# q and k in tiles of 256, 256 and three times 512 tokens in a fused attention and gMLP kernel, with E's zeros partly on ScalarE and a new order

## The chip, the cores and the metric

The kernel runs on one core of a Trainium2 chip. Its engines are TensorE (PE; its weight loads PEld), VectorE (DVE), ScalarE (ACT), GpSimd (POOL) and SyncE (SP), which issues all of this kernel's DMAs; each takes its instructions in the order in which they were written, and they wait for each other by semaphores. The metric is the device time of one execution in microseconds (us), as a median of several runs.

## The reference

One sequence of 2048 tokens with 448 channels goes through two blocks with residuals. The first is attention of 16 heads of 28 channels, where each token looks at 8 positions: itself and those 2, 4, ... 14 back. The second is a gMLP: a GELU layer of 2 x 896 channels, whose second half is normalised and mixed over all tokens by a 2048 x 2048 matrix. All data is bf16.

```python
qkv = layernorm(x) @ wqkv                   # 448 -> 3*448
idx = pos[:, None] - 2 * arange(8)          # masked where negative
attn = softmax(q . k[idx] * 28 ** -0.5)
h = x + (attn . v[idx]) @ wo
z = gelu(layernorm(h) @ w_in)               # 448 -> 1792
z1, z2 = z[:, :896], layernorm(z[:, 896:])
out = h + (z1 * (w_sp @ z2 + b_sp)) @ w_out
```

## The kernel before

The tokens lie in 16 blocks of 128 (`x_tm`). Each block is normalised on VectorE (statistics L634 and L636, GpSimd's rstd L628 and L629, `xn` L645) and transposed into `xhT`: the first four blocks (`xT0` to `xT3`) by TensorE (L674) with an eviction (`xe`), the others by a transposing DMA.

q and k come from `product` (L502), in 5 tiles of tokens (`QT`) times 4 groups of heads (`make_qk`, job `qk<tile>_<group>`). A product has 14 matmuls on half the rows of the array, in two jobs A (8) and B (6) with another job between them, and takes two of the 8 PSUM banks: k in one, q in the other. `qe` copies k to `kT` (L512), `qf` copies q to `qd` twice, each time with other rows masked by `qm` (ScalarE, L723), or in one instruction on VectorE (L726). Weights come packed: `wraw` is loaded in two halves, and ten copies `wp` bring it into `wqk` (L512), where GpSimd has zeroed the gaps (`wpad`, L695). `kT` and `qd` are a ring of 1592 tokens; tile 4 is written over the first tokens' places once blocks 0 to 4 have been used, and blocks 14 to 17 of the attention read it there.

The attention has 18 blocks of 112 to 128 queries. For each: logits `lg` (L814, 16 matmuls), exponentials `ex` into one of four slots of `E` (ScalarE, L824 and L825), a mask product `mk` (VectorE, L832), the product with the values `o` (L845, two jobs of 16), reciprocal and scaling (`rc`, `om`, L862 and L865) into `otm`, a small copy `od`, and a transposing DMA into `OT`. Values are products too (`v`, 14 matmuls of 448 columns, for two blocks), evicted by `ve`. E's unused halves must be zero: `pads0` to `pads3` (L598 and L599) write them once. Blocks 11 to 17 need one more copy `oc` behind their DMA.

Then `y` (with wo), the residual `h` (L775), the second normalisation, z1 and z2 (L502 again, 512 and 448 columns; GELU at L946, L902 and L905; `z2c` evicts z2 where its GELU comes later), the token mixing `g` (L974, 448 matmuls of 512 columns from `wsp_la`, `wsp_lb`, `wsp_hi`, which transposing DMAs bring), bias and product with z1 (L983, L986), the output product `wo` (L998), the last residual (L1005) and 16 stores.

No scheduler runs when the kernel is built: every job has a number, `ORDER` lists all numbers in the order in which they are given out (926 is a filler matmul, L1013, that keeps TensorE busy), `BANK` the PSUM banks, and `ON` the engine of the jobs that have a choice. `Sched.issue` derives the waits from what each instruction reads and writes.

Of the kernel before, what the change touches and what calls it, by code (L numbers as in the profile page):

```python
# [1073 lines left out]
```

## Time and profile before

| what | us |
|---|---|
| median of 3 runs | 241.84 (241.83 to 242.95) |
| the profiled execution: its time | 242.61 |
| its span | 240.9 |
| TensorE busy | 230.7 |
| VectorE, ScalarE, GpSimd busy | 147.3, 92.5, 32.4 |

The granted TensorE clock is 1.00 throughout. A line of the profile names a source line, an engine and an operation with its result and operands; a matmul's busy time reaches to its modelled end, so that neighbours overlap. Timeline lines begin with start and length; a bracket at the end gives the idle time before the line and what ended it.

### The profile page before, as it was taken

What the parts mean: (1) busy time and instruction counts of PE and PEld (TensorE: products, weight loads), DVE (VectorE), ACT (ScalarE), POOL (GpSimd) and SP (SyncE); (2) the same over time, 40 slices, a digit from 0 to 9 for tenths busy, and PEclk for the clock granted to TensorE, in tenths of its full rate; (3) what the DMA queues carried; (4) which work ended last, traced back from release to release, by engine and by line L of the source; (5) the groups of instructions that cost most, each with busy time, mean ns of one, the idle gap of its engine ahead of it and who ended that gap; (6) DMA issues with size and microseconds to landing.
All of it is one profiled execution on the core that took longest, in us unless ns stands there. A gap on an engine that the chain in (4) does not pass through costs nothing.

```text
span 240.9 us, 5622 instructions
## 1 busy us (share of the span) xinstructions
PE 230.7 (96%) x2394; PEld 115.7 (48%) x2406; DVE 147.3 (61%) x335; ACT 92.5 (38%) x132; POOL 32.4 (13%) x80
## 2 busy tenths in 40 slices
PE   7769899999999999999999999999999999999995
PEld 2536555555565554444444444444444434444443
DVE  6997787889997969677794044620311741052844
ACT  2588958868789474989800000000000000000000
POOL 5553210111132030303333000000000000000000
...
GB/s 181 373 80 103 90 112 71 135 197 118 114 110 132 114 135 182 95 180 171 180 191 198 189 105 3 0 0 0 3 1 0 0 38 3 0 19 19 38 79 114
DMA packets 66313, 23.31 MB, mean 97 GB/s; under 512 B 58608, under 2 KB 66160, under 8 KB 66288
## 3 DMA queue, kind: packets, MB, share of 16 engines
...
q8 instruction: 19, 0.31, 0.6%
...
## 4 chain that ended last, share of the span: by engine, by line
PE 87%; DVE 6%; ACT 5%; issue 1%; POOL 0%; POOLq 0%
PE psum L974 37%; PE psum L502 35%; PE psum L998 9%; PE psum L845 3%; ACT qd L723 2%; PE psum L814 2%; DVE ub L983 2%; DVE z1p L986 1%; ACT kT L512 1%; PE psum L1013 1%; DVE E L598 1%; DVE st L634 1%; ACT E L824 1%; DVE x_tm L775 0%; ACT xhT L512 0%
## 5 line engine op out<-in xcount | busy, mean ns | idle before, releaser
L983 DVE TENSOR_TENSOR ub<-psum,bb 128x512 bf16<-128x512 f32 x28 | 19.3, 690 | 56.1 <-PE psum L974 55.8
L974 PE MATMUL psum<-wsp_hi,z2p 128*128 128x512 bf16 x217 | 50.1, 379 | 0.7 <-DVE srg L1005 0.4
L974 PEld LDWEIGHTS psum<-wsp_hi,z2p 128*128 128x128 bf16 x224 | 21.8, 98 | 26.9 <-DVE srg L1005 0.6
L502 PE MATMUL psum<-xhT,wqk 64*128 64x512 bf16 (+3 forms) x280 | 27.4, 335 | 0.0
L974 PE MATMUL psum<-wsp_la,z2p 128*128 128x512 bf16 x110 | 26.4, 379 | 0.3 <-issue 0.2
L974 PE MATMUL psum<-wsp_lb,z2p 128*128 128x512 bf16 x110 | 26.2, 379 | 0.1
L502 PE MATMUL psum<-w_in,hnT 64*128 64x448 bf16 x224 | 24.1, 349 | 0.0
L502 PE MATMUL psum<-hnT,w_in 64*128 64x512 bf16 x196 | 24.0, 376 | 0.0
L998 PE MATMUL psum<-w_out,z1p 128*128 128x448 bf16 (+1 forms) x119 | 22.8, 342 | 0.1
L909 DVE BATCH_NORM_STATS2 st<-z2p 128x6 f32<-128x448 bf16 x32 | 18.5, 612 | 1.6 <-ACT z2p L905 1.4
L723 ACT ACTIVATE qd<-psum,qm 128x512 bf16<-128x512 f32 (+3 forms) x34 | 18.1, 615 | 3.5 <-PE psum L502 3.4
L634 DVE BATCH_NORM_STATS2 st<-x_tm 128x6 f32<-128x448 bf16 x32 | 19.0, 611 | 0.1
L825 ACT ACTIVATE E<-psum 128x1024 bf16<-128x1024 f32 x17 | 17.0, 1031 | 1.3 <-PE psum L814 0.7
L974 PEld LDWEIGHTS psum<-wsp_lb,z2p 128*128 128x128 bf16 x112 | 10.9, 98 | 13.2
L974 PEld LDWEIGHTS psum<-wsp_la,z2p 128*128 128x128 bf16 x112 | 10.9, 98 | 13.3 <-DVE mv L912 0.4
L629 POOL TENSOR_TENSOR rs<-rs,negh 128x2 f32<-128x2 f32 (+2 forms) x22 | 16.9, 767 | 1.8
L502 PE MATMUL psum<-wv,xhT 64*128 64x448 bf16 x126 | 15.0, 351 | 1.9 <-ACT kT L512 1.9
L998 PEld LDWEIGHTS psum<-w_out,z1p 128*128 128x128 bf16 x119 | 11.5, 98 | 10.4 <-DVE z1p L986 0.4
L1005 DVE TENSOR_TENSOR srg<-psum,x_tm 128x448 bf16<-128x448 f32 (+1 forms) x17 | 9.7, 593 | 10.9 <-PE psum L998 9.3
L502 PEld LDWEIGHTS psum<-xhT,wqk 64*128 64x128 bf16 x280 | 12.3, 94 | 8.3 <-DVE wqk L512 0.4
L502 PEld LDWEIGHTS psum<-w_in,hnT 64*128 64x128 bf16 x224 | 10.7, 94 | 10.5 <-ACT z1p L946 0.2
L645 DVE TENSOR_SCALAR xn<-x_tm,mv,rs 128x512 bf16<-128x512 bf16 x32 | 12.5, 416 | 4.6 <-POOL rs L629 3.9
(65 smaller groups left out, 238.3 us busy)
## 6 DMA issues: line engine op xcount, KB each, us to landing
...
out_dram<-srg SPq DMA_DIRECT2D x16, 112.0 KB, 1.7
...
```

The source lines that it names most:

```text
L502: ins = e.matmul(out(k), w(k, p0, c), x(k, p0, c), start=(k, p0, c) in first, stop=(k, p0, c) in last, tile_position=(p0, 0))
L629: (lambda e: e.tensor_tensor(R, A, negh[:, 0:1].to_broadcast([128, n]), ALU.pow), [rr, r_negh], r_rs[k][m:m + n])],
L634: [(lambda e: e.bn_stats(st[:, m, :], src), [rsrc], [r_st[k][m]])], dve_t(D))
L645: [(lambda e: e.tensor_scalar(xn[:, s, :].rearrange("p (a b) -> p a b", a=2), bass.AP(x_tm[:].tensor, m * D, [[NB * D, 128], [192, 2], [1, ...
L723: return e.activation(qd[:, g, i, a:a + n], psv(tk, 0, n), AF.Copy, scale=qm[:, i:i + 1])
L825: return e.activation(o[:, :, :, 0:64], psum[:, tk.b * 512:tk.b * 512 + 1024].rearrange("p (i h q) -> p i h q", i=2, q=64), AF.Exp, scale= ...
L845: ins = e.matmul(psum[:, c:c + DH + 1], E[64 * r:64 * r + 64, slot, a:a + 128], V1[64 * r:64 * r + 64, vs, 4 * (2 * k + gg) + hh, 0:DH + 1 ...
L909: [(lambda e, m=m, k=k: e.bn_stats(st3[:, m, k, :], z2p[:, m, D * k:D * (k + 1)]), [r_z2[m]], [r_st[2][m]])], dve_t(D))
L974: ins = e.matmul(psv(tk), z2p[:, s, 128 * fc:128 * fc + 128], w[:, 512 * (tc % 2):512 * (tc % 2) + 512], start=(s == 0), stop=(s == NB - 1))
L983: [(lambda e, tc=tc, s=s, tk=tk: e.tensor_tensor(ub[:, s, :], psv(tk), bb[:, 512 * tc:512 * tc + 512], ALU.add), [r_bb], [r_ub[s]])], dve_ ...
L998: ins = e.matmul(psv(tk, 0, c1 - c0), z1p[:, fc, 128 * m:128 * m + 128], w_out[:, fc, c0:c1], start=(fc == 0), stop=(fc == FC7 - 1))
L1005: [(lambda e, m=m, s=s, tk=tk, c0=c0, c1=c1: e.tensor_tensor(srg[:, s, c0:c1], psv(tk, 0, c1 - c0), x_tm[:, m, c0:c1], ALU.add), [r_x[m]], ...
```

## The change

- The tiles of q and k are tokens 0, 256, 512, 1024 and 1536 onwards, 256, 256, 512, 512 and 512 wide. Before, they began at 0, 256, 568, 1080 and 1578, and were 256, 312, 512, 512 and 470 wide. Tile 1 now needs token blocks 2 and 3 alone, where it needed block 4 too.
- Tile 4 now begins inside the part of the ring that isn't reused: its first 56 tokens go to their own places, 1536 to 1591, for block 13 of the attention, and its tokens from 1578 on go to the ring's start. So each of its evictions is two instructions, of 470 and of 56 columns, and 14 of its columns are written twice.
- E's zeros may be written by ScalarE, as an activation with scale 0 of `warm`: `pads0` and `pads1` are now there, `pads2` on GpSimd, `pads3` on VectorE. Before, three were on VectorE and `pads1` on GpSimd.
- `ORDER`, `BANK` and `ON` are new tables. By `ON`, VectorE now has q of tile 0, group 3, k of tile 1, group 0 and q of tile 1, group 1, five evictions of z2 (`z2c`) where it had one, one eviction of the values (`ve12`), and `od0` to `od4`, `od7`, `od12`, `od14`, `od16` and `od17`.

There are now 16 fillers where there were 21. SyncE's first 13 loads stand as before.

TensorE from its first instruction. `warm` is the filler's operand, `ident` and `xn` those of a transpose, `xhT` and `wqk` those of q and k, `wv` of the values, `qd` and `kT` of the logits. Before:

```order
1 L1013 MATMUL psum<-warm 128x512 x12
2 L674 MATMUL psum<-ident,xn 128x128 x8
3 L1013 MATMUL psum<-warm 128x512 x7
4 L502 MATMUL psum<-xhT,wqk 128x256 x56
5 L1013 MATMUL psum<-warm 128x512
6 L502 MATMUL psum<-wv,xhT 128x448 x8
7 L674 MATMUL psum<-ident,xn 128x128 x8
8 L502 MATMUL psum<-wv,xhT 128x448 x6
9 L1013 MATMUL psum<-warm 128x512
10 L502 MATMUL psum<-wv,xhT 128x448 x8
11 L814 MATMUL psum<-qd,kT 64x2x78 x8
```

The same place now:

```order
1 L1036 MATMUL psum<-warm 128x512 x8
2 L682 MATMUL psum<-ident,xn 128x128 x4
3 L1036 MATMUL psum<-warm 128x512
4 L682 MATMUL psum<-ident,xn 128x128 x4
5 L1036 MATMUL psum<-warm 128x512 x7
6 L502 MATMUL psum<-xhT,wqk 128x256 x56
7 L682 MATMUL psum<-ident,xn 128x128 x8
8 L502 MATMUL psum<-wv,xhT 128x448 x8
9 L502 MATMUL psum<-xhT,wqk 128x256 x30
10 L502 MATMUL psum<-wv,xhT 128x448 x6
11 L502 MATMUL psum<-xhT,wqk 128x256 x26
12 L502 MATMUL psum<-wv,xhT 128x448 x8
```

The second pair of transposes (rows 7) moved ahead of all value products, and the whole second tile of q and k stands among them, without fillers.

VectorE from its first instruction. `st_62` and `mv_63` are the statistics of the first normalisation, `rs_68` its rstd. Before:

```order
1 L588 MEMSET warm 128x512
2 L603 MEMSET otm 128x512
3 L598 MEMSET E 128x16x32
4 L599 MEMSET E 128x32
5 L598 MEMSET E 128x16x32
6 L599 MEMSET E 128x32
7 L601 MEMSET qm 128x2
8 L602 MEMSET qm 32x1 x4
9 L634 BN_STATS st_62<-x_tm 128x6
10 L636 BN_AGGR mv_63<-st_62 128x2
11 L634 BN_STATS st_62<-x_tm 128x6
12 L636 BN_AGGR mv_63<-st_62 128x2
```

The same place now:

```order
1 L588 MEMSET warm 128x512
2 L642 BN_STATS st_62<-x_tm 128x6
3 L644 BN_AGGR mv_63<-st_62 128x2
4 L642 BN_STATS st_62<-x_tm 128x6
5 L644 BN_AGGR mv_63<-st_62 128x2
6 L653 TENSOR_SCALAR xn<-x_tm,mv_63,rs_68 128x512 x2
7 L603 MEMSET E 128x16x32
8 L603 MEMSET E 128x32
9 L512 COPY wqk<-wraw 128x2x8x28 x2
10 L611 MEMSET otm 128x512
11 L512 COPY wqk<-wraw 128x2x4x28 x3
12 L609 MEMSET qm 128x2
```

The statistics of blocks 0 and 1 moved to the head; one slot of E, otm and qm are cleared behind them, among the copies of the weights. Behind this come the statistics of blocks 3, 2, 7 and 5, the normalisation of blocks 2 and 3, statistics of 4 and 6, and then q of tile 0, group 3.

ScalarE at the evictions of tile 4, with the exponentials (`E`) of blocks 8 and 12 at its two ends. Before, its four groups stood apart:

```order
35 L723 ACTIVATE qd<-psum,qm 128x470 x2
36 L512 ACTIVATE kT<-psum 128x470
37 L825 ACTIVATE E<-psum 128x16x64
38 L512 ACTIVATE V_81<-psum 128x32x28
39 L825 ACTIVATE E<-psum 128x16x64 x3
40 L512 ACTIVATE V_81<-psum 128x32x28
41 L825 ACTIVATE E<-psum 128x16x64
42 L512 ACTIVATE V_81<-psum 128x32x28
43 L512 ACTIVATE kT<-psum 128x470
44 L723 ACTIVATE qd<-psum,qm 128x470 x4
45 L512 ACTIVATE kT<-psum 128x470
46 L825 ACTIVATE E<-psum 128x16x64
```

Now:

```order
43 L848 ACTIVATE E<-psum 128x16x64 x3
44 L731 ACTIVATE kT<-psum 128x470
45 L731 ACTIVATE kT<-psum 128x56
46 L737 ACTIVATE qd<-psum,qm 128x470 x2
47 L737 ACTIVATE qd<-psum,qm 128x56 x2
48 L731 ACTIVATE kT<-psum 128x470
49 L731 ACTIVATE kT<-psum 128x56
50 L737 ACTIVATE qd<-psum,qm 128x470 x2
51 L737 ACTIVATE qd<-psum,qm 128x56 x2
52 L731 ACTIVATE kT<-psum 128x470
53 L731 ACTIVATE kT<-psum 128x56
54 L848 ACTIVATE E<-psum 128x16x64
```

Two groups and the k of a third now come in a row between exponentials, each with its pieces of 56 columns; that group's q and the fourth group follow the last row shown.

The diff, cut to its core:

```diff
-ORDER = [21, 45, 22, 28, 23, 25, 30, 0, 31, 32, 27, 46, 33, 121, 47, 1, 53, 54, 44, 48, 34, 49, 2, 26, 124, 55, 56, 926, 926,
+ORDER = [21, 45, 30, 0, 44, 46, 24, 47, 22, 31, 32, 33, 1, 53, 54, 48, 23, 55, 2, 121, 123, 49, 56, 26, 122, 124, 926, 926,
...
-QT = [(0, 256), (256, 568), (568, 1080), (1080, 1592), (1578, 2048)]
+QT = [(0, 256), (256, 512), (512, 1024), (1024, 1536), (1536, 2048)]
...
-        r_qk = [[spot("qk%d_%d" % (t, g), o_qk, 12 * SL * 2) for g in range(12)] for t in range(len(QT))]
+        r_qk = [[spot("qk%d_%d" % (t, g), o_qk, 12 * SL * 2) for g in range(24 if t == 4 else 12)] for t in range(len(QT))]
...
-            move_z("pads%d" % i, [(lambda e, i=i: e.memset(ez(i), 0.0), [], [r_Ez[i]]),
+            def zero(e, o, act):
+                if act:
+                    x = warm[:, 0:64]
+                    return e.activation(o, x if len(o.shape) == 2 else x.unsqueeze(1).to_broadcast([128, NHEAD, 64]), AF.Copy, scale=0.0)
+                return e.memset(o, 0.0)
+            za = ON.get("pads%d" % i) == "act"
...
-                move("qe%d_%d" % (t, g), "act", ekey, lambda n=n, a=a, g=g: kT[:, g, a:a + n], lambda n=n, tk=tk: psv(tk, 1, n),
...
+                parts = [(0, lo, n)] if t < 4 else [(1578 - lo, 0, hi - 1578), (0, lo, SL - lo)]
+
+                def ke(e, part, eng, g=g, tk=tk):
+                    c, a, w = part
+                    o, x = kT[:, g, a:a + w], psv(tk, 1, 512)[:, c:c + w]
+                    return e.activation(o, x, AF.Copy) if eng == "act" else e.tensor_copy(o, x)
+
+                def qe(e, part, i, eng, g=g, tk=tk):
+                    c, a, w = part
+                    x = psv(tk, 0, 512)[:, c:c + w]
+                    if eng == "act":
+                        return e.activation(qd[:, g, i, a:a + w], x, AF.Copy, scale=qm[:, i:i + 1])
+                    return e.tensor_tensor(qd[:, g, :, a:a + w], x.unsqueeze(1).to_broadcast([128, 2, w]),
+                                           qm[:].unsqueeze(2).to_broadcast([128, 2, w]), ALU.mult)
...
-                if (t == 4 if b >= 14 else t < 4 and lo < t0 + nq and hi > t0 - pad):
+                if (t == 4 if b >= 14 else lo < t0 + nq and hi > t0 - pad):
```

More of the change, by code (lines that the diff above doesn't have):

```diff
@@ L25 @@
 LOOK = {'pe': 0.009410205530073946, 'act': 1e-09, 'dve': 0.19498114580727732, 'pool': 1e-09, 'sp': 0.13408016923274957}
-ORDER = [21, 45, 22, 28, 23, 25, 30, 0, 31, 32, 27, 46, 33, 121, 47, 1, 53, 54, 44, 48, 34, 49, 2, 26, 124, 55, 56, 926, 926,
[40 rows of a table removed]
-BANK = [2, 0, 4, 5, 4, 6, 2, 0, 2, 6, 0, 4, 6, 2, 0, 6, 4, 0, 4, 0, 0, 0, 4, 0, 6, 4, 2, 6, 4, 0, 2, 2, 0, 6, 6, 0, 2, 4, 4,
[3 rows of a table removed]
+ORDER = [21, 45, 30, 0, 44, 46, 24, 47, 22, 31, 32, 33, 1, 53, 54, 48, 23, 55, 2, 121, 123, 49, 56, 26, 122, 124, 926, 926,
[40 rows of a table added]
+BANK = [0, 2, 0, 1, 2, 0, 4, 6, 6, 0, 0, 2, 2, 4, 6, 6, 0, 2, 2, 6, 4, 6, 0, 0, 2, 4, 4, 0, 4, 0, 0, 4, 2, 6, 0, 6, 2, 4, 0,
[3 rows of a table added]
     7]
@@ new lines @@
+ON = {'pads0': 'act', 'pads1': 'act', 'pads2': 'pool', 'pads3': 'dve', 'xe0_0': 'act', 'xe0_1': 'act', 'xe1_0': 'act',
+    'xe2_0': 'act', 'xe3_0': 'act', 'wp0_0_0': 'dve', 'wp0_1_0': 'act', 'wp0_0_2': 'dve', 'wp0_1_2': 'act', 'wp1_0_0':
+    'dve', 'wp1_1_0': 'dve', 'wp1_0_1': 'dve', 'wp1_1_1': 'act', 'wp1_0_2': 'act', 'wp1_1_2': 'act', 'qe0_0': 'act',
[4 rows of a table added]
+    'qf3_2': 'dve', 'qe3_3': 'act', 'qf3_3': 'act', 've0': 'act', 'padsx': 'dve', 'od0': 'dve', 'od1': 'dve', 've2':
+    'act', 'od2': 'dve', 'od3': 'dve', 've4': 'act', 'od4': 'dve', 'od5': 'pool', 've6': 'act', 'qe4_0': 'act',
+    'qf4_0': 'act', 'qe4_1': 'act', 'qf4_1': 'act', 'qe4_2': 'act', 'qf4_2': 'act', 'qe4_3': 'act', 'qf4_3': 'act',
+    'od6': 'pool', 'od7': 'dve', 've8': 'act', 'od8': 'pool', 'od9': 'pool', 've10': 'act', 'od10': 'pool', 'od11':
+    'pool', 'oc11': 'dve', 've12': 'dve', 'od12': 'dve', 'oc12': 'dve', 'od13': 'pool', 'oc13': 'dve', 've14': 'act',
+    'od14': 'dve', 'oc14': 'act', 'od15': 'pool', 'oc15': 'act', 've16': 'act', 'od16': 'dve', 'oc16': 'act', 'od17':
+    'dve', 'oc17': 'dve', 'z2c1': 'dve', 'z2c2': 'dve', 'z2c3': 'act', 'z2c4': 'dve', 'z2c5': 'act', 'z2c6': 'act',
+    'z2c7': 'dve', 'z2c8': 'act', 'z2c9': 'dve', 'z2c10': 'act', 'z2c13': 'act'}
@@ L597, in bass_sequential_preLN__sliding_local_dilated__mixer_gmlp__prompt_kernel @@
         for i in range(NE):
-            move_z("pads%d" % i, [(lambda e, i=i: e.memset(ez(i), 0.0), [], [r_Ez[i]]),
-                                  (lambda e, i=i: e.memset(E[:, i, NHEAD * 128:NHEAD * 128 + 64], 0.0), [], [r_Ez[i]])], {"dve": 0.65, "pool": 1.3})
+            def zero(e, o, act):
[4 more added lines that the diff above has]
+            za = ON.get("pads%d" % i) == "act"
+            move_z("pads%d" % i, [(lambda e, i=i, za=za, zero=zero: zero(e, ez(i), za), [r_warm], [r_Ez[i]]),
+                                  (lambda e, i=i, za=za, zero=zero: zero(e, E[:, i, NHEAD * 128:NHEAD * 128 + 64], za), [r_warm], [r_Ez[i]])],
+                   {"dve": 0.6, "pool": 1.1, "act": 1.05})
         r_qm = Res("qm")
@@ L705, in make_qk @@
             lo, hi = QT[t]
-            n, a = hi - lo, lo if t < 4 else 0
+            n = hi - lo
             for g in range(4):
@@ L716, in make_qk @@
                 ekey = lo / 112.0 + KEY["qe"] + KEY["qkg"] * g
-                move("qe%d_%d" % (t, g), "act", ekey, lambda n=n, a=a, g=g: kT[:, g, a:a + n], lambda n=n, tk=tk: psv(tk, 1, n),
-                     [], [r_qk[t][3 * g]] + [r_qk[o][3 * g] for o in also], evac_t(n), [tk], (tk, 1, 1))
-                name = "qf%d_%d" % (t, g)
-                eng = ON.get(name, "act")
-                def fa(e, i, n=n, a=a, g=g, tk=tk):
-                    return e.activation(qd[:, g, i, a:a + n], psv(tk, 0, n), AF.Copy, scale=qm[:, i:i + 1])
@@ L725, in fv @@
-                def fv(e, n=n, a=a, g=g, tk=tk):
-                    return e.tensor_tensor(qd[:, g, :, a:a + n], psv(tk, 0, n).unsqueeze(1).to_broadcast([128, 2, n]),
-                                           qm[:].unsqueeze(2).to_broadcast([128, 2, n]), ALU.mult)
-                wr = [[r_qk[o][3 * g + 1 + i] for o in (t,) + tuple(also)] for i in range(2)]
-                ops = [(lambda e, i=i, fa=fa: fa(e, i), [r_qm], wr[i]) for i in range(2)] if eng == "act" else [(fv, [r_qm], wr[0] + wr[1])]
@@ new lines, in qe @@
+                def qe(e, part, i, eng, g=g, tk=tk):
[5 more added lines that the diff above has]
+                                           qm[:].unsqueeze(2).to_broadcast([128, 2, w]), ALU.mult)
+                for name, bank in (("qe", 1), ("qf", 0)):
+                    name = "%s%d_%d" % (name, t, g)
+                    eng = ON.get(name, "act")
+                    ops, durs = [], {"act": 0.0, "dve": 0.0}
+                    for ip, part in enumerate(parts):
+                        w = part[2]
+                        wr = [[r_qk[t][12 * ip + 3 * g + i]] + [r_qk[o][3 * g + i] for o in also if ip == 0] for i in range(3)]
+                        if bank:
+                            ops.append((lambda e, part=part, eng=eng, ke=ke: ke(e, part, eng), [], wr[0]))
+                            durs = {"act": durs["act"] + act_t(w), "dve": durs["dve"] + dve_t(w)}
+                        else:
+                            ops += [(lambda e, part=part, i=i, eng=eng, qe=qe: qe(e, part, i, eng), [r_qm], wr[1 + i] if eng == "act" else wr[1] + wr[2])
+                                    for i in (range(2) if eng == "act" else [0])]
+                            durs = {"act": durs["act"] + 2 * act_t(w) + 0.187, "dve": durs["dve"] + dve_t(2 * w)}
+                    j = pl.job(name, eng, ekey, ops, durs[eng], use=[tk], rel=(tk, bank, 1))
+                    j.alts = durs
```

14 lines of the change are left out of this document (removed), and 94 rows, old and new, of tables (BANK, ON, ORDER).

## The prediction

> **What bounds the kernel now.** I read the page first, then busy time by stretch, then the timeline of the first 30 us and the groups of instructions.
>
> ```profile
> span 240.9 us, 5622 instructions
> PE 230.7 (96%) x2394; PEld 115.7 (48%) x2406; DVE 147.3 (61%) x335; ACT 92.5 (38%) x132; POOL 32.4 (13%) x80
> PE   7769899999999999999999999999999999999995
> ```
>
> TensorE is busy nearly throughout; what is missing stands in the first five slices of 6 us. The next view gives stretches: start and end, length, then busy us of PE, PEld, DVE, ACT and POOL.
>
> ```profile
> 9.78:30.00 20.22, 17.04 (x318) 10.76 (x320) 16.29 (x46) 17.62 (x37) 7.21 (x17) 1.00 0.48 123
> 30.00:119.70 89.70, 89.21 (x1498) 47.27 (x1496) 74.46 (x170) 70.33 (x88) 14.97 (x34) 1.00 0.81 137
> 119.70:238.40 118.70, 117.58 (x556) 54.99 (x565) 48.69 (x97) 1.24 (x2) 4.15 (x8) 1.00 0.24 49
> 48.00:72.00 24.00, 23.60 (x558) 13.68 (x554) 22.32 (x53) 18.38 (x25) 4.04 (x10) 1.00 0.71 134
> ```
>
> From 30 us to the last matmul, 208.4 us, TensorE idles 1.6 us. So a new order can gain there next to nothing; it can gain only ahead of 30 us, and it can lose anywhere. The front, engine by engine (start, length, engine, line, what; in brackets what the engine waited for):
>
> ```profile
> 1.51 4.78 PE L1013 MATMUL psum<-warm 128*128 128x512 bf16 x12 [1.51 <-DVE warm L588]
> 7.72 0.62 PE L674 MATMUL psum<-ident,xn 128*128 128x128 bf16 x8 [1.42 <-DVE xn L645]
> 8.18 1.67 PE L1013 MATMUL psum<-warm 128*128 128x512 bf16 x7
> 9.78 3.23 PE L502 MATMUL psum<-xhT,wqk 64*128 64x256 bf16 x56
> 14.41 0.93 PE L502 MATMUL psum<-wv,xhT 64*128 64x448 bf16 x8 [1.39 <-ACT kT L512]
> 17.57 0.39 PE L1013 MATMUL psum<-warm 128*128 128x512 bf16 x1 [1.01 <-ACT qd L723]
> 19.95 3.87 PE L502 MATMUL psum<-xhT,wqk 64*128 64x312 bf16 x56
> ```
>
> Real work starts with the first q/k tile at 9.78. Up to 30 us the idle time is 20.22 - 17.04 = 3.2 us, and the filler at 17.57 hides another 0.3: 3.5 us of holes. The two large ones come after the first q/k tile: all eight banks hold its products, and TensorE waits until ScalarE has emptied them (kT, qd); the second q/k tile, which could fill the time, needs token block 4, which comes late through a transposing DMA.
>
> **The change, part by part.** The sum is made against the profiled execution's 242.61 us (span 240.9, 1.7 around it); the median of the runs is 241.84, 0.77 lower, and I take the same difference off both.
>
> *When real work starts.* The rows on which this rests:
>
> ```profile
> 0.79 0.87 SPq L527 DMA_DIRECT2D x_tm<-in_A_x_dram  x2
> DMA to landing us min/median/max: 2.1/5.7/6.9
> 3.91 0.63 DVE L634 BATCH_NORM_STATS2 st<-x_tm 128x6 f32<-128x448 bf16 x1
> 5.77 0.41 DVE L645 TENSOR_SCALAR xn<-x_tm,mv,rs 128x512 bf16<-128x512 bf16 x1 [0.29 <-POOL rs L629]
> 6.88 0.64 POOL L605 MEMSET V<- 128x96 bf16 x1
> 6.98 0.68 DVE L645 TENSOR_SCALAR xn<-x_tm,mv,rs 128x512 bf16<-128x512 bf16 x1
> 7.76 0.95 POOL L598 MEMSET E<- 128x1024 bf16 x1
> L512 DVE COPY wqk<-wraw x5: 242/264/957, 6.8 to 9.4; 128x448 bf16<-128x448 bf16 x4, 128x224 bf16<-128x224 bf16 x1
> L598 DVE MEMSET E<- 128x512 uint32 x3 | 1.5, 485 | 0.2
> 7.94 0.86 ACT L512 ACTIVATE wqk<-wraw 128x224 bf16<-128x224 bf16 x2 [5.66 <-DMA wraw<-in_A_wqkv_dram]
> L825 ACT ACTIVATE E<-psum 128x1024 bf16<-128x1024 f32 x17 | 17.0, 1031 | 1.3 <-PE psum L814 0.7 <-PE psum L845 0.5
> ```
>
> Before, VectorE clears otm, two slots of E and qm ahead of the first statistics, which start at 3.91. Now they start when x lands, 0.8 + 2.1 = 2.9, and the first xn, which ends 2.3 us after that start (5.77 + 0.41 - 3.91), ends at 5.2; the second one GpSimd round later, at about 6.3 (5.77 to 6.98 is such a round). Then VectorE clears one slot of E (0.5 and a small memset: to 6.9) and packs wqk. In that time GpSimd, whose rstd ends near 5.7, has the memset of wqk's gaps, a mask step and the clearing of slot 2 (0.95) in its queue, so that this last one runs from about 6.7 to 7.7. In the rows an xn of 0.41 takes 0.68 under one GpSimd memset and a copy of 0.26 takes 0.96 under the other: I take the first copy as held until 7.8. The second ends at 8.1, otm's memset at 8.6, and the three small copies (0.24 each; the second half of wraw has landed at 7.9) at 9.35. The first product needs two of them: 9.2. Without the hold it would be 8.6, the other bound; the third bound is no gain, 9.8. I take 9.2, the row that shows a copy under this very memset: **-0.6** (-1.2 to 0). ScalarE's two clearings (1.03 each by the E row of the same 1024 columns, and small ones) run from 2.3 (7.94 - 5.66) to about 4.8, inside its 5.66 of waiting; uncovered they would cost 2.5.
>
> *The fillers.* The same filler takes 4.78/12 = 0.40 at first and 1.67/7 = 0.24 later, with a granted clock of 1.00 in both, so the column doesn't show this. Now 8 run ahead of the first transposes, ending near 4.9, with short waits of 0.3 behind; I count that as warm enough (0). The Trainium skill, "TensorE: Matmul & The Clock Gate", Part 1, says the array runs at half rate until a free-running window of about 3.4 us was busy, and that the moment differs between runs. By that rule 8 fillers might not be enough; that is a rival below.
>
> *The holes behind the first tile.* The rows:
>
> ```profile
> 9.58 0.61 DVE L634 BATCH_NORM_STATS2 st<-x_tm 128x6 f32<-128x448 bf16 x1
> 11.54 0.72 POOL L629 TENSOR_TENSOR rs<-rs,negh 128x2 f32<-128x2 f32 x1
> 11.64 1.57 ACT L723 ACTIVATE qd<-psum,qm 128x256 bf16<-128x256 f32 x4 [1.06 <-PE psum L502]
> 13.08 1.23 ACT L512 ACTIVATE kT<-psum 128x256 bf16<-128x256 f32 x4
> 15.70 1.08 ACT L512 ACTIVATE xhT<-psum 128x512 bf16<-128x512 f32 x2 [0.67 <-PE psum L674]
> L983 DVE TENSOR_TENSOR ub<-psum,bb 128x512 bf16<-128x512 f32 x28 | 19.3, 690 | 56.1 <-PE psum L974 55.8
> ```
>
> The second tile is now tokens 256 to 511, which TensorE itself transposes, so its 56 matmuls (3.2) stand where the holes were. First hole: the first tile ends at 9.2 + 3.2 = 12.4. VectorE sets qm (0.5 after 9.35) and starts the statistics of blocks 2 and 3 at 9.9; from that start to their rstd it is 11.54 + 0.72 - 9.58 = 2.7, so 12.6; their xn may again meet a GpSimd memset (V's ones are next there): 13.3. Hole 0.9, at best 0.3. The transposes, their eviction (two in 1.08) and the first value product last to 14.8; a q/k product to 15.3. Second hole: the next one's banks hold the first tile's group 3, whose q now leaves by VectorE, behind two normalisations, two statistics of 0.6 and four aggregations: from 15.2 to 15.9 (0.69 by the row of the like read of PSUM). Hole 0.65. Behind that ScalarE's queue (0.39 for a qd, 0.31 for a kT by the two rows above) is one step ahead of or behind TensorE; I count 0.65 of small waits at the first logits and the third value product. In all 2.2 for 3.5: **-1.3**; bounds -2.3 (0.3, 0.6 and small ones of 0.3) and 0 (as many holes as before).
>
> *Columns.* Three widths of 56 matmuls are in rows:
>
> ```profile
> 113.40 6.21 PE L502 MATMUL psum<-hnT,w_in 64*128 64x512 bf16 x56
> ```
>
> 3.23, 3.87 and 6.21 for 256, 312 and 512 are 12.1 to 12.6 ns a column, so 14 columns fewer are **-0.2**. Two more separate groups of logits (14 for 12) put back **+0.1**, by the 0.42 below against their 0.29 in pairs; both within ±0.3.
>
> *Tile 4.* Its eviction writes 470 columns and then 56 again: 12 more instructions on ScalarE. And its four groups now stand close together. From the logits of block 8 on, ScalarE has three exponentials and all four groups before the logits of block 13 can run; value and output products wait behind those on TensorE.
>
> ```profile
> L512 ACT ACTIVATE kT<-psum 128x470 bf16<-128x470 f32 x4 | 2.2, 562 | 0.4 <-PE psum L502 0.4
> L723 ACT ACTIVATE qd<-psum,qm 128x470 bf16<-128x470 f32 x8 | 4.8, 650 | 1.7 <-PE psum L502 1.7
> L512 ACT ACTIVATE wqk<-wraw 128x224 bf16<-128x224 bf16 x3 | 1.2, 388 | 5.7 <-DMA wraw<-in_A_wqkv_dram 5.7
> 27.07 1.96 ACT L825 ACTIVATE E<-psum 128x1024 bf16<-128x1024 f32 x2
> 53.41 1.49 PE L502 MATMUL psum<-wv,xhT 64*128 64x448 bf16 x14
> 52.85 0.42 PE L814 MATMUL psum<-qd,kT 64*64 64x128 bf16 x16
> 66.72 0.99 PE L845 MATMUL psum<-V,E 64*128 64x29 bf16 x64
> ```
>
> TensorE meanwhile has 3.4 q/k groups (6.21/4 each: 5.3), three products of 1.45, one logits (0.4) and four blocks of 32 E matmuls (0.5 each by 0.99 for 64): about 12. ScalarE: 3 x 1.03 + 4 x 0.56 + 8 x 0.65 = 10.5, less 0.1 an instruction where they follow each other (two exponentials of 1.03 take 1.96), plus 12 small ones. No row has 56 columns. A kT takes in sequence 0.46 for 470 columns (0.56 less 0.1) and 0.31 for 256 (1.23/4), 0.7 ns a column, which leaves 0.17 for 56; the upper bound is the 0.39 of 224 columns. So 10.5 - 1.5 + 2.0 = 11 against 12: covered, **0**; upper bound 10.5 + 4.7 = 15.2, a wait of 3.2.
>
> *Everything else* moves banks, engines and queue places at stretches where TensorE idles 1.6 in 208: one value eviction, four evictions of z2 and two small copies more go to VectorE, which idles 89.70 - 74.46 = 15.2 there, while SyncE's queue keeps its first 13 loads. **0**, from -0.4 (half of today's late holes gone) to +1.4.
>
> Sum: -0.6 - 1.3 - 0.2 + 0.1 = **-2.0**: 242.61 becomes 240.6, and the median 241.84 becomes **239.8**.
>
> **The rivals.**
>
> *Better.* The copies aren't held and the holes shrink to their lower bounds: -1.2 - 2.3 - 0.1 = -3.6, 238.2; more likely half-way, 238.7. Chance 0.10.
>
> *Cold array.* If the wait ahead of the transposes keeps the array slow for one more window, the 7 later fillers take 2.8 instead of 1.7 from 6.6 on and end at 9.4, and part of the first tile runs at 0.40/0.24 of its time: 0.3 to 1.4, say 0.8. Result 240.6. For it: the ratio in the rows. Against: 8 fillers are 3.2 us, nearly the whole of the 4 or so that 12 needed. Chance 0.08.
>
> *VectorE takes the lead back.* Between 48 and 72 us it is busy 22.32 of 24. An added eviction of 896 columns there costs 1.06:
>
> ```profile
> L512 DVE CAST z2p<-psum 128x896 bf16<-128x896 f32 x1 | 1.1, 1057 | 0.0
> ```
>
> If the whole of it and two small copies (0.15 each) reach TensorE, 1.4 of 2.0 is lost: 241.2, no change. Against: by the sums above VectorE has done by 30 us what it does today by then, and four evictions of q and k more (0.4 to 1.2 each), so it has a lead of its own. Chance 0.14.
>
> *ScalarE is late with tile 4* (slower). Where a small piece costs its full 0.39 and nothing overlaps, block 13's logits wait 3.2; where ScalarE enters that place with 1 us of arrears, 4.2, and the result is 239.8 + 3.2 to 4.2, 243.0 to 244.0, say 243.5. It decides from about 0.35 a piece on; below 0.2 it costs nothing. For it: ScalarE has little slack there, 18.4 busy of 24, and gets 2 to 4.7 us more. Chance 0.10.
>
> **How the numbers follow.** The forecast, with its own range of 239.0 to 240.6, has 0.58. A measurement of this kernel tells 0.5%, 1.2 us, from no change: faster than 240.63 are the forecast and the better case, 0.68; within, the cold array and VectorE, 0.22; slower, ScalarE, 0.10. The range of 8 in 10 leaves out the far side of the better case and the slower one: 238.3 to 242.0.
>
> **What would show it.** Right: the first q/k product starts between 8.6 and 9.4; TensorE has 1.5 to 2.5 us of holes from there to 30 us, the first before the transposes of blocks 2 and 3, the second before a q/k product that waits for VectorE's qd; a piece of 56 columns shows under 0.3; from 30 us on TensorE idles under 2. Wrong: fillers at 0.40 behind 6 us; matmuls of L837 or of values waiting for ScalarE's kT or qd of 56 columns; waits for VectorE at E's products above 1 us; or a first tile that starts no earlier than 9.8.

## The result and the profile after

The changed kernel takes 241.35 us (median of 13 runs, 239.48 to 243.81) beside 242.33 us (13 runs, 241.83 to 242.95) for the kernel before on the same chip: ratio 0.9937, 95% interval 0.9915 to 0.9960, 1.5 us less. (Four of its runs, at 243.4 to 243.8 with a mean granted clock of 0.993, are left out of the ratio; with them, the medians stand at 0.9960, 1.0 us less.) Run again later on another chip it had 0.9953 (0.9927 to 0.9979). The prediction was 239.8 us, a gain of 2.0, in a range of 238.3 to 242.0. The profiled execution took 241.03 us, 1.58 less than before. Its page:

```profile
span 239.3 us, 5622 instructions
PE 230.0 (96%) x2401; PEld 115.9 (48%) x2401; DVE 151.7 (63%) x339; ACT 91.7 (38%) x141; POOL 30.8 (13%) x77
```

The stretches, as before (start and end, length, busy us of PE, PEld, DVE, ACT and POOL, granted clock):

```profile
8.41:30.00 21.59, 19.09 (x336) 11.60 (x338) 19.15 (x55) 17.38 (x36) 6.49 (x17) 1.00 0.55 142
30.00:119.70 89.70, 88.19 (x1484) 47.41 (x1479) 80.36 (x181) 66.45 (x93) 16.11 (x35) 1.00 0.79 137
119.70:236.70 117.00, 116.99 (x563) 54.71 (x561) 46.78 (x90) 1.69 (x2) 2.81 (x6) 1.00 0.23 48
```

Up to 30 us TensorE idles 21.59 - 19.09 = 2.5 us, where it had 3.5 us of holes. But in the middle stretch it now idles 1.5 us, where it had 0.5. The timeline of TensorE says where (in brackets the idle time ahead of a row and what ended it):

```profile
6.52 1.67 PE L1036 MATMUL psum<-warm 128*128 128x512 bf16 x7
8.41 3.23 PE L502 MATMUL psum<-xhT,wqk 64*128 64x256 bf16 x56 [0.22 <-DVE wqk L512]
12.46 0.83 PE L682 MATMUL psum<-ident,xn 128*128 128x128 bf16 x8 [0.82 <-DVE xn L653]
15.08 1.37 PE L502 MATMUL psum<-xhT,wqk 64*128 64x256 bf16 x22 [0.44 <-DVE qd L738]
20.96 0.93 PE L502 MATMUL psum<-wv,xhT 64*128 64x448 bf16 x8 [0.29 <-ACT E L848]
23.82 1.04 PE L502 MATMUL psum<-xhT,wqk 64*128 64x512 bf16 x8 [0.91 <-ACT E L848]
49.60 1.04 PE L502 MATMUL psum<-xhT,wqk 64*128 64x512 bf16 x8 [1.10 <-DMA xhT<-xn]
```

The first q/k product starts at 8.41 instead of 9.78. Four holes follow. And at 49.60 stands a wait that the kernel before doesn't have: tile 4's first product waits 1.10 us for a transposing DMA. SyncE's queue shows the reason (start, time that the queue was taken):

```profile
40.64 3.59 SPq L526 DMA_TRANSPOSE OT<-otm  x2
44.28 2.58 SPq L526 DMA_TRANSPOSE xhT<-xn  x2
```

The transposes of blocks 15 and 14 (`xhT<-xn`) stand behind those of outputs 3 and 4 (`OT<-otm`), which VectorE has to write first. In the kernel before, blocks 12 to 15 stood ahead of output 2, and the last three of them went out here:

```profile
35.46 5.33 SPq L526 DMA_TRANSPOSE xhT<-xn  x3
```

Next, VectorE at the head of the changed kernel, and ScalarE's groups of the small pieces:

```profile
2.90 0.63 DVE L642 BATCH_NORM_STATS2 st<-x_tm 128x6 f32<-128x448 bf16 x1 [1.45 <-DMA x_tm<-in_A_x_dram]
6.89 0.73 DVE L512 COPY wqk<-wraw 128x448 bf16<-128x448 bf16 x2
9.00 0.63 DVE L642 BATCH_NORM_STATS2 st<-x_tm 128x6 f32<-128x448 bf16 x1
```

```profile
L737 ACT ACTIVATE qd<-psum,qm 128x56 bf16<-128x56 f32 x8 | 2.2, 365 | 0.0
L731 ACT ACTIVATE kT<-psum 128x56 bf16<-128x56 f32 x4 | 1.0, 258 | 0.0
```

The statistics of block 0 start when x lands, and those of blocks 2 and 3 at 9.00 instead of 9.58. Two milestones split the time: the first product with the spatial weights (118.54; before 119.77) and the end of the last matmul. Here are the rows of after, then of before:

```profile
118.54 1.69 PE L997 MATMUL psum<-wsp_la,z2p 128*128 128x512 bf16 x7
228.48 8.21 PE L1021 MATMUL psum<-w_out,z1p 128*128 128x448 bf16 x49
```

```profile
119.77 1.46 PE L974 MATMUL psum<-wsp_la,z2p 128*128 128x512 bf16 x6 [0.16 <-issue]
230.07 8.22 PE L998 MATMUL psum<-w_out,z1p 128*128 128x448 bf16 x49
```

From the first q/k product to the first milestone it is 109.99 before and 110.13 after: what the smaller holes bring, the new wait takes. From there to the end of the last matmul it is 118.52 and 118.15. So the 1.6 us are 1.37 at the start and 0.4 late, less 0.1 between.

### The profile page after: what moved, and what is told of

It is laid out like the page before. It is cut to its first block, busy times and chain, and to the rows that moved or that the text cites. A ratio compares the mean times of both kernels' runs of the same rounds, so it can differ in the third digit from the quotient of the medians.

```text
span 239.3 us, 5622 instructions
## 1 busy us (share of the span) xinstructions
PE 230.0 (96%) x2401; PEld 115.9 (48%) x2401; DVE 151.7 (63%) x339; ACT 91.7 (38%) x141; POOL 30.8 (13%) x77
## 3 DMA queue, kind: packets, MB, share of 16 engines
HBM read 6.83 MB, written 1.84 MB: 36 GB/s over the span
## 4 chain that ended last, share of the span: by engine, by line
PE 77%; DVE 11%; ACT 5%; DMA 2%; POOL 2%; issue 1%; SPq 1%; POOLq 0%; DVEq 0%
PE psum L997 40%; PE psum L502 24%; PE psum L1021 9%; DVE st L642 3%; PE psum L868 2%; PE psum L837 2%; DMA xhT<-xn 2%; POOL rs L637 2%; DVE xn L653 1%; DVE x_tm L798 1%; ACT z1p L969 1%; DVE otm L888 1%; DMA x_tm<-in_A_x_dram 1%; DVE z2p L512 1%; ACT qd L737 1%
## 5 line engine op out<-in xcount | busy, mean ns | idle before, releaser
L997 PE MATMUL psum<-wsp_hi,z2p 128*128 128x512 bf16 x224 | 51.8, 379 | 0.0
L502 PE MATMUL psum<-xhT,wqk 64*128 64x512 bf16 (+1 forms) x280 | 28.0, 334 | 2.7 <-DMA xhT<-xn 1.1
L997 PE MATMUL psum<-wsp_la,z2p 128*128 128x512 bf16 x112 | 25.7, 379 | 0.0
L737 ACT ACTIVATE qd<-psum,qm 128x256 bf16<-128x256 f32 (+3 forms) x38 | 17.8, 555 | 2.3 <-PE psum L502 2.1
L969 ACT ACTIVATE z1p<-psum 128x1024 bf16<-128x1024 f32 x14 | 13.9, 1023 | 12.1 <-PE psum L502 12.1
L868 PEld LDWEIGHTS psum<-V,E 64*128 64x128 bf16 x576 | 12.2, 93 | 6.9 <-DVE otm L888 0.4
```

The costliest lines, as they stand in the source:

```text
L502: ins = e.matmul(out(k), w(k, p0, c), x(k, p0, c), start=(k, p0, c) in first, stop=(k, p0, c) in last, tile_position=(p0, 0))
L737: return e.activation(qd[:, g, i, a:a + w], x, AF.Copy, scale=qm[:, i:i + 1])
L868: ins = e.matmul(psum[:, c:c + DH + 1], E[64 * r:64 * r + 64, slot, a:a + 128], V1[64 * r:64 * r + 64, vs, 4 * (2 * k + gg) + hh, 0:DH + 1 ...
L969: return e.activation(o, i, AF.Gelu_apprx_tanh)
L997: ins = e.matmul(psv(tk), z2p[:, s, 128 * fc:128 * fc + 128], w[:, 512 * (tc % 2):512 * (tc % 2) + 512], start=(s == 0), stop=(s == NB - 1))
```

## The experiments

The ratios are to runs of the kernel before on the same chip: e1 to e4 ran on one chip, e5 to e8 on a second, e9 to e12 on a third. Only the second has the unaltered changed kernel beside the others (e5), so differences between groups are less sure than those within one. The line numbers of these kernels are up to two lower than the changed kernel's. In the orders, xT is the transposing DMA of a block of x (on TensorE for blocks 0 to 3), oT that of an output, n0, st0 and mv0 are normalisation, statistics and aggregation, pads the clearing of a slot of E, wp a copy of weights, qe and qf the evictions of k and q, rc, om, od the normalising of an output, mk a mask step, lg logits, v a value product.

| kernel | median us | ratio to before (95%) |
|---|---|---|
| changed kernel, first | 241.35 | 0.9937 (0.9915 to 0.9960) |
| e1 transposes early on SyncE | 242.12 | 0.9974 (0.9949 to 0.9999) |
| e2 old head in the changed kernel | 241.54 | 0.9970 (0.9940 to 1.0000) |
| e3 clearing moved in the kernel before | 242.80 | 1.0001 (0.9975 to 1.0027) |
| e4 wide pieces doubled | 247.72 | 1.0200 (1.0163 to 1.0236) |
| e5 changed kernel again | 241.39 | 0.9953 (0.9927 to 0.9979) |
| e6 SyncE's queue relieved | 240.57 | 0.9915 (0.9886 to 0.9944) |
| e7 otm and qm cleared early | 240.55 | 0.9903 (0.9873 to 0.9934) |
| e8 both of these | 239.78 | 0.9874 (0.9836 to 0.9912) |
| e9 second tile late | 242.24 | 0.9977 (0.9953 to 1.0001) |
| e10 one q back on ScalarE | 241.75 | 0.9956 (0.9929 to 0.9982) |
| e11 small pieces doubled | 243.59 | 1.0018 (0.9985 to 1.0051) |
| e12 both, and a shorter head | 240.80 | 0.9919 (0.9891 to 0.9946) |

**What tile 4 waits for: e1 and e6.** My theory after the result was the place in SyncE's queue; the rival, that the wait only moves. e1 changes the places alone:

```diff
 SyncE
-oT0 w_in0_0 w_in3_1 xT13 w_in2_1 oT1 oT2 w_in0_1 xT12 oT3 oT4 xT15 xT14
+oT0 w_in0_0 xT15 w_in3_1 xT13 w_in2_1 oT1 oT2 xT14 w_in0_1 xT12 oT3 oT4
```

> The changed kernel with one thing moved: the two transposing DMAs of token blocks 15 and 14 stand on SyncE's queue right behind the normalisations that feed them, ahead of those of the outputs 1, 3 and 4 which they followed. Theory (queue place): TensorE's 1.10 us wait for xhT ahead of tile 4 comes from that place alone; it goes, tile 4's first product starts by about 48.7 instead of 49.60 and everything behind moves with it: ratio to the kernel before 0.988 to 0.991 where the changed kernel has 0.9937. Rival (the wait moves on): TensorE only waits elsewhere between 46 and 60 us, for the output transposes 3 and 4 that now come some 3 us later, or for ScalarE's exponentials: ratio 0.993 to 0.996 and a new wait of about 1 us there.

The rival's mechanism holds. The wait for xhT is gone, and TensorE waits for output transposes instead, 1.35 at 48.33 and 0.56 at 64.13. With 1.91 of waiting in place of 1.10 the ratio, 0.9974, lies above even the rival's range. The first of the two rows:

```profile
48.33 0.93 PE L501 MATMUL psum<-wo,OT 64*128 64x448 bf16 x8 [1.35 <-DMA OT<-otm]
```

So it isn't one transpose that is late but the queue that is full: each transpose takes it for 1.2 us and each load of w_in for about 0.6. Block 14's normalisation isn't the cause: in the changed kernel it ends at 39.75, and the queue takes the two transposes only from 44.28 on. e6 takes four loads out of that stretch, moves the transposes of the last blocks ahead of output 3, and has block 14 normalised early enough for that:

```diff
 VectorE
-n0_12 qf3_2 rc2 om2 od2 mk4 mk5 qe3_0 rc3 om3 n0_14 od3
+n0_12 n0_14 qf3_2 rc2 om2 od2 mk4 mk5 qe3_0 rc3 om3 od3
 SyncE
-oT0 w_in0_0 w_in3_1 xT13 w_in2_1 oT1 oT2 w_in0_1 xT12 oT3 oT4 xT15 xT14 oT5
+oT0 xT15 xT13 oT1 xT12 oT2 xT14 oT3 w_in0_0 w_in3_1 oT4 w_in2_1 w_in0_1 oT5
```

> The changed kernel with SyncE's queue relieved ahead of tile 4: block 14 is normalised right behind block 12 (its input has been ready since 27 us), the transposes of blocks 13, 15, 12 and 14 go out behind their normalisations and all ahead of that of output 3, and four loads of w_in move behind the transposes of outputs 3 and 4. Theory (SyncE's queue is what tile 4 waits for): neither xhT at 49.6 nor the output transposes of the first experiment at 48.3 and 64.1 are waited for; TensorE's idle time between 30 and 72 us falls from 1.2 to under 0.3, ratio 0.988 to 0.991. Rival (ScalarE has no slack at tile 4, as the doubling of its wide pieces showed): TensorE comes 1.1 us earlier to products and logits that wait for ScalarE's exponentials or for banks that it empties, ratio 0.993 to 0.996 and those waits in place of the DMA's.

Beside it on that chip ran the changed kernel unaltered:

> The changed kernel itself, unaltered, so that the next three have it beside them on the same chip: ratio to the kernel before 0.992 to 0.996, as measured at first.

It had 0.9953, e6 0.9915: 0.9 us less, by intervals that overlap a little (e6's reaches up to 0.9944, e5's down to 0.9927). The trace carries it: TensorE is busy for all of the 12 us in which tile 4 starts (changed kernel: 10.90), and no wait for ScalarE has come in place of the DMA's.

```profile
48.00:60.00 12.00, 12.00 (x268) 6.92 (x264) 10.74 (x25) 10.60 (x25) 2.41 (x6) 1.00 0.36 89
```

**What sets the pace of the front: e2, e3, e7, e12.** e2 puts VectorE's clearing back ahead of the statistics in the changed kernel:

```diff
 VectorE
-wset st0_0 mv0_0 st0_1 mv0_1 n0_0 n0_1 pads3 wp0_0_0 wp0_0_2 otmz wp1_0_0 wp1_0_1 wp1_1_0 qmz st0_3
+wset otmz pads0 pads3 qmz st0_0 mv0_0 st0_1 mv0_1 n0_0 n0_1 wp0_0_0 wp0_0_2 wp1_0_0 wp1_0_1 wp1_1_0 st0_3
-ON = {'pads0': 'act', ...
+ON = {'pads0': 'dve', ...
```

> The changed kernel with VectorE's clearing put back ahead of the first statistics (otm, two slots of E, one of them taken back from ScalarE, and qm). Theory A (the prediction's: what stands ahead of the statistics sets when real work starts): statistics at 3.9 instead of 2.9, the first q/k product at 9.3 to 9.8 instead of 8.41, time up by 0.9 to 1.4 against the changed kernel, ratio 0.9975 to 0.9995. Theory B (the second half of the q/k weights, which lands at about 7.9, and the copies behind it set the start): the first-half copies still fit ahead of the landing, the first q/k product at 8.5 to 8.9, time up by 0.1 to 0.5, ratio 0.994 to 0.996.

The first product starts at 9.15, between the two theories. The rows show why, and something neither had:

```profile
7.52 1.67 PE L1035 MATMUL psum<-warm 128*128 128x512 bf16 x7
9.15 3.33 PE L501 MATMUL psum<-xhT,wqk 64*128 64x256 bf16 x56
12.42 0.78 PE L681 MATMUL psum<-ident,xn 128*128 128x128 bf16 x8
23.70 1.04 PE L501 MATMUL psum<-xhT,wqk 64*128 64x512 bf16 x8 [0.88 <-ACT E L847]
8.91 0.61 DVE L641 BATCH_NORM_STATS2 st<-x_tm 128x6 f32<-128x448 bf16 x1
```

The seven fillers behind block 1's transposes take 1.67 us, and the first product follows their end (9.19), as it does in the kernel before (8.18 + 1.67 = 9.85) and, but for 0.22, in the changed one. And the later start costs nothing in the front: the hole of 0.82 ahead of the second transposes is gone, and at 23.7 TensorE is 0.12 ahead of the changed kernel. In both, VectorE starts the statistics of blocks 2 and 3 at 8.9 to 9.0. That points to this chain as what paces the front. The ratio (0.9970) is above the changed kernel's, but the intervals overlap widely; what the trace loses, it loses at tile 4, where the wait is 1.52 instead of 1.10.

e3 gives the kernel before the same move of the clearing, and nothing else of the new head:

```diff
 VectorE
-wset otmz pads0 pads2 qmz st0_0 mv0_0 st0_1 ... wp0_1_2 st0_3
+wset st0_0 mv0_0 st0_1 ... wp0_1_2 otmz qmz st0_3
 ScalarE
-tbl wp1_0_1
+tbl pads0 pads2 wp1_0_1
```

> The kernel before with two slots of E cleared by ScalarE instead of VectorE and otm and qm cleared behind the weight copies, so that its first statistics start at 2.9 as in the changed kernel; its order of weight copies, which engine makes them, and everything else are the old ones. Theory A (clearing ahead of the statistics sets the start): first q/k product at 8.4 to 8.8 instead of 9.78, and 0.9 to 1.3 faster if the holes behind the first tile don't grow, ratio 0.994 to 0.996. Theory B (landing of the second half of the weights at 7.9 and the four wide copies and an eviction that the old order has behind it): first product at 9.2 to 9.7, gain 0.1 to 0.5, ratio 0.998 to 1.0. In either case holes that wait for ScalarE's evictions of the first tile can take the gain back: then the first product is early and TensorE's idle time from there to 30 us is larger than 3.2 by as much.

```profile
9.12 3.23 PE L501 MATMUL psum<-xhT,wqk 64*128 64x256 bf16 x56
35.98 1.04 PE L501 MATMUL psum<-xhT,wqk 64*128 64x512 bf16 x8 [0.92 <-DMA xhT<-xn]
9.92 0.63 DVE L640 BATCH_NORM_STATS2 st<-x_tm 128x6 f32<-128x448 bf16 x1
```

The first product comes at 9.12, at the end of the fillers as in e2, 0.66 earlier. In this order its holes don't grow (at 23.00 there stands what stood at 23.66), so up to there the front does follow the first product. Then a wait of 0.92 for a transposing DMA takes it back at 36 us. The same product in the kernel before:

```profile
35.56 1.02 PE L502 MATMUL psum<-xhT,wqk 64*128 64x512 bf16 x8
```

It is 0.42 later in e3, and the chain of normalisations is 0.34 later too: the statistics of blocks 2 and 3 start at 9.92 instead of 9.58, because otm and qm now stand ahead of them. This move alone is worth nothing (1.0001).

e7 moves only the two clearings that stand in VectorE's chain into an idle time ahead of it:

```diff
 VectorE
-wset st0_0 ... wp0_0_2 otmz wp1_0_0 wp1_0_1 wp1_1_0 qmz st0_3
+wset qmz otmz st0_0 ... wp0_0_2 wp1_0_0 wp1_0_1 wp1_1_0 st0_3
```

> The changed kernel with otm and qm cleared by VectorE between its first memset and the landing of x (it idles there), so the statistics of blocks 2 and 3 start some 0.5 us earlier; the first q/k product keeps its 8.4. Theory (the front runs at the pace of VectorE's normalisations, not of the first product): the hole ahead of the second pair of transposes falls from 0.8 to 0.3, TensorE is 0.4 to 0.5 us ahead at 23 us. What becomes of it: if tile 4's transposes follow TensorE's own progress, through the outputs that precede them in SyncE's queue, it is kept: ratio 0.002 below the unaltered changed kernel. Rival: the wait for xhT at 49.6 grows by as much, or ScalarE's evictions behind the first tile take it: same time as the unaltered one, within 0.001.

```profile
7.93 0.61 DVE L641 BATCH_NORM_STATS2 st<-x_tm 128x6 f32<-128x448 bf16 x1
6.83 1.17 DVE L511 COPY wqk<-wraw 128x448 bf16<-128x448 bf16 x5
```

```profile
8.20 3.33 PE L501 MATMUL psum<-xhT,wqk 64*128 64x256 bf16 x56
22.79 1.04 PE L501 MATMUL psum<-xhT,wqk 64*128 64x512 bf16 x8 [0.95 <-ACT E L847]
48.96 1.04 PE L501 MATMUL psum<-xhT,wqk 64*128 64x512 bf16 x8 [1.48 <-DMA xhT<-xn]
```

The chain starts 1.07 earlier (9.00 to 7.93, more than the 0.5 expected), TensorE is 1.03 ahead at 22.8, and the time is 1.2 us less (0.9903 beside 0.9953, by intervals that just overlap). Of this the trace shows 0.64 at tile 4 (48.96 for 49.60), since the wait for xhT grows to 1.48. The first product came only 0.2 earlier. Together with e2 this settles it for the changed kernel: the normalisations set the pace of the front, not the first product. e8 has e6 and e7 together:

> Both of the two alterations before in one kernel. If each saves its own stretch the savings add: ratio 0.986 to 0.989. If one path (ScalarE's evictions) lies just under both, together they save no more than one of them alone: 0.990 to 0.993.

```profile
46.57 0.93 PE L501 MATMUL psum<-wo,OT 64*128 64x448 bf16 x8 [0.40 <-DMA OT<-otm]
```

Ahead of tile 4 a wait of 0.40 is left. The two savings add up within the noise: 0.0079 below the unaltered kernel, where the two alone have 0.0038 and 0.0050. At 0.9874 (0.9836 to 0.9912), 3.1 us below the kernel before, it beats both kernels. e12 tries for more:

```diff
 VectorE
-n0_0 n0_1 pads3 wp0_0_0 ... mv0_5 qf0_3 st0_10
+n0_0 n0_1 wp0_0_0 ... mv0_5 qf0_3 pads3 st0_10
 TensorE
-xT1 warm x7
+xT1 warm x4
```

> The kernel with both alterations and two more at the head: slot 3 of E is cleared behind the first tile's eviction on VectorE instead of ahead of the weight copies (0.64), and three of the seven fillers that stand ahead of the first q/k product are gone (0.24 each). Theory (VectorE's chain of copies and normalisations paces the front, and the fillers only have to end before it): the first q/k product starts at 7.5 to 8.0, the statistics of blocks 2 and 3 start up to 0.6 earlier, 0.3 to 0.6 faster than with both alterations alone: ratio 0.985 to 0.987. Rival (ScalarE, which works without a pause from 15 to 23.5 us, sets the pace behind): what is won at 12 us is lost in waits for its exponentials at 20 and 23 us: ratio 0.987 to 0.989.

```profile
6.14 1.84 DVE L511 COPY wqk<-wraw 128x448 bf16<-128x448 bf16 x5
```

```profile
8.14 3.33 PE L501 MATMUL psum<-xhT,wqk 64*128 64x256 bf16 x56 [0.60 <-ACT wqk L511]
23.31 1.04 PE L501 MATMUL psum<-xhT,wqk 64*128 64x512 bf16 x8 [1.37 <-DMA xhT<-xn]
```

Neither theory. The copies start 0.7 earlier than in e7 and end at the same time: they now lie beside GpSimd's memset of a slot from its start (1.84 for the five, 1.17 in e7). So the chain starts no earlier (6.14 + 1.84 = 7.98), the memset of slot 3 now lies inside it (0.64 at 13.98), and block 4's transpose and those behind it come late (1.37 of wait at 23.3). The fillers left out bring 0.06: the product then waits for weights. The ratio is 0.9919, 0.0045 above e8's on another chip, and the intervals overlap; so e12 shows no gain, and its loss is read from the trace.

**What fills the holes: e9, e10.** e9 keeps the tiles of 256 and puts the second tile's products where the old order had them. Their evictions move along on ScalarE and VectorE, and three products use other banks:

```diff
 TensorE
-xT2 xT3 v0A qk1_2A qk1_0A qk1_2B qk1_3A v0B qk1_3B qk1_1A qk1_0B qk1_1B v2A lg1_0 v2B lg0_1 lg0_0 v4A
+xT2 v0A xT3 v0B v2A lg1_0 v2B lg0_1 lg0_0 qk1_2A qk1_0A qk1_2B qk1_3A qk1_0B qk1_1A qk1_3B qk1_1B v4A
```

> The changed kernel (tiles of 256, 256, 512) with the second q/k tile put back to where the old order has it on TensorE: behind the value products 0 and 2 and the logits of blocks 0 and 1, with ScalarE's and VectorE's evictions in the same order and three products in other banks. Theory (the second tile, placed right behind the transposes of blocks 2 and 3, fills the time in which the first tile's banks are emptied): without it TensorE again waits for banks and for ScalarE's qd; idle time from the first product to 30 us is 3.2 to 4.0 instead of 2.5, and the time is up by 0.7 to 1.5 against the changed kernel: ratio 0.997 to 1.001 where that has 0.9937 and 0.9953. Rival (the sum of ScalarE's and VectorE's work up to 25 us sets the pace, whatever TensorE's order): the holes only change places, within 0.4 us: ratio 0.993 to 0.996.

```profile
8.40:30.00 21.60, 18.20 (x311) 10.88 (x312) 17.99 (x51) 16.70 (x35) 5.92 (x15) 1.00 0.54 140
```

```profile
18.23 0.61 PE L500 MATMUL psum<-xhT,wqk 64*128 64x256 bf16 x8 [0.95 <-ACT V L510]
19.39 2.79 PE L500 MATMUL psum<-xhT,wqk 64*128 64x256 bf16 x48 [0.56 <-ACT E L845]
23.07 0.93 PE L500 MATMUL psum<-wv,xhT 64*128 64x448 bf16 x8 [0.88 <-ACT kT L729]
```

The theory holds by the trace: the holes up to 30 us are 3.3 (21.6 less 18.20 busy and 0.12 ahead of the first product) instead of 2.5. The time goes the same way, 0.9977, which is 0.6 to 1.0 us more than the changed kernel (0.9953 and 0.9937), but the intervals overlap. So the place of the second tile is worth some 0.8 us of holes, about half of the gain; as a difference in time this isn't clear of the noise. e10 undoes VectorE's share in the first tile's evictions:

```diff
-ON = {... 'qf0_3': 'dve', ...
+ON = {... 'qf0_3': 'act', ...
 ScalarE
-qe0_2 qe0_3 xe2_0 xe3_0 qf0_0
+qe0_2 qe0_3 qf0_3 xe2_0 xe3_0 qf0_0
```

> The changed kernel with one eviction moved back: q of the first tile's group 3 leaves by ScalarE (two instructions of 0.42 behind its k) instead of VectorE. Theory (sharing of the first tile's evictions with VectorE is part of the gain): ScalarE is 0.8 later with the transposed blocks 2 and 3 and with group 0, TensorE's wait of 0.44 for VectorE's qd goes but one of 0.6 to 0.9 for ScalarE's xhT comes ahead of it: 0.2 to 0.6 slower, ratio 0.995 to 0.997. Rival (ScalarE idles 1.08 us at 16, so it can take it): the 0.44 goes and nothing comes, ratio 0.992 to 0.994.

```profile
23.81 1.04 PE L501 MATMUL psum<-xhT,wqk 64*128 64x512 bf16 x8 [1.16 <-DMA xhT<-xn]
```

The wait for VectorE's qd is gone, and at 23.81 TensorE stands where it stood (23.82), now waiting for a transposing DMA. The ratio, 0.9956, lies in the theory's range, but that was set against 0.9937; beside e5's 0.9953 it is the same. So the time decides nothing, and by the trace the hole ahead of VectorE's qd cost nothing by 24 us.

**ScalarE at tile 4: e4, e11.** e4 was meant to double the small pieces; the first entry of the list is the wide one, so it doubled the twelve of 470 columns:

```diff
-parts = [(0, lo, n)] if t < 4 else [(1578 - lo, 0, hi - 1578), (0, lo, SL - lo)]
+parts = [(0, lo, n)] if t < 4 else [(1578 - lo, 0, hi - 1578), (0, lo, SL - lo), (1578 - lo, 0, hi - 1578)]
```

> The changed kernel with each of tile 4's twelve 56-column instructions issued twice on ScalarE: the pieces' cost is doubled, everything else is the same. Theory (pieces are cheap and covered): each takes some 0.15 in sequence, 1.8 us of ScalarE in all, of the 4.3 that it idles between 48 and 72 us; no TensorE wait for kT or qd comes, ratio within 0.001 of the changed kernel's 0.9937. Rival (ScalarE is at its limit at tile 4): TensorE waits for exponentials or for tile 4's banks by 1 to 2 us, ratio 0.997 to 1.002.

```profile
L737 ACT ACTIVATE qd<-psum,qm 128x470 bf16<-128x470 f32 x16 | 9.6, 685 | 0.0
```

This group was busy 4.9 us in the changed kernel, and that of k is 4.7 instead of 2.4. From 53 us on, ScalarE's rows of tile 4 last 15.4 us where they lasted 9.2, 6.2 more, and TensorE waits for it four times, 1.38, 1.15, 0.83 and 1.69, 5.05 in all: about 1.2 to spare. It says nothing of the small pieces; e11 doubles those:

```diff
+parts = [(0, lo, n)] if t < 4 else [(1578 - lo, 0, hi - 1578), (0, lo, SL - lo), (0, lo, SL - lo)]
```

> The changed kernel with tile 4's pieces of 56 columns, twelve on ScalarE, issued twice, and its wide pieces once (the earlier run had doubled the wide ones). In sequence a small piece adds 0.15 to 0.25, so 1.8 to 3.0 us of ScalarE. Theory (the wide ones' run: 6.3 us added there, some 5 came out as TensorE's waits, so ScalarE has about 1.3 to spare): 0.5 to 1.7 of it reaches TensorE as waits for qd, kT or an exponential between 52 and 70 us; ratio 0.996 to 1.001. Rival (the small pieces are covered, as predicted): no such wait, ratio 0.993 to 0.996.

```profile
56.52 1.04 PE L502 MATMUL psum<-xhT,wqk 64*128 64x512 bf16 x8 [0.44 <-ACT qd L737]
65.48 0.42 PE L837 MATMUL psum<-qd,kT 64*64 64x128 bf16 x16 [0.75 <-ACT kT L731]
```

Here, too, TensorE waits (these and 0.22 at 59.2), 1.4 us of some 2.4 added, and the time is 1.0018, beyond the upper end of what I expected: 1.6 to 2.0 us above the changed kernel. Issued once, the pieces are covered, with about 1 us to spare.

## Why the prediction came out as it did

The direction and the range were right, and the gain does begin ahead of 30 us. The size was 0.5 too large. That the sum came this close is partly luck: the front brought 2.4 us where I had 1.9, and a wait of 1.1 us that the sum didn't have took the difference and more.

- *When real work starts, -0.6*: mis-sized, -1.37, outside my bounds. I had the first weight copy held by GpSimd until 7.8 and the product at 9.2, at best 8.6. Such a hold exists: in e2 and e12, where the copies start ahead of GpSimd's memset, one of them takes 1.10. Here they start 0.57 behind it, the longest takes 0.52, and the product came at 8.41, behind the fillers and 0.22 of waiting. What the step missed is e2's lesson: a start 0.74 later shortened the first hole by 0.82. The start by itself is no gain in this order; only its sum with the holes counts, -2.4 where I had -1.9.
- *The holes, -1.3*: 2.5 us instead of 2.2, so -1.0. The first stood where I said and was nearly as long (0.82 for 0.9), the second too but shorter (0.44 for 0.65), and two waits for ScalarE's exponentials (0.29 and 0.91) are larger than the 0.65 I gave to small ones. The cause that I named, the second tile in place of the holes, is borne out by e9's trace with 0.8; the chain of normalisations, which I used only to place the first hole, is shown by e2 and e7 as the pace of the front behind it.
- *The fillers, 0*: right. Those behind 6 us take 1.67/7 = 0.24 each; the cold array did not come.
- *Tile 4, 0*: right in the changed kernel, where no wait for kT or qd stands behind 49.60; in sequence a small piece takes about 0.25 for k and 0.18 for q (e11 against the rows of after), near my 0.17. By itself a piece of q shows 0.365, above the 0.3 that I named as a sign, and one of k 0.258. My margin was 11 against 12, and e4 and e11 find about as much to spare: 1.0 to 1.2 us over twelve pieces, so the rival's case would have begun at about 0.3 a piece in sequence, where I put it at 0.35.
- *Everything else, 0*: this step failed. I wrote that "SyncE's queue keeps its first 13 loads" and looked no further down that queue. Its later part puts the transposes of blocks 15 and 14 behind outputs that wait for VectorE, and that is a wait of 1.1 us that the sum had at nothing, more than the 0.5 by which the gain falls short. e6 takes it away and has 0.9915 of the 242.3 us, 240.3, which is the gain that I forecast. Against it, the 0.38 that TensorE had waited for srg (VectorE's last residual, L1005) late in the kernel before is gone.
- *VectorE takes the lead back*: at the forecast's price the result, 0.9937 of 242.33, 240.8, lies near this rival's 241.2, but the wait it names isn't there: no product waits for VectorE between 48 and 72 us.

What stays open: how the 1.5 us divide between the second tile's place and the earlier chain, since e9's 0.8 and the chain's 0.58 (9.58 to 9.00) belong to different surroundings and the differences in time are near the noise; and what of the change in the order gave the 0.4 late in the kernel, which no run here undid.
